# A decode step's tail: w_down's last rows laid out without zeros, the last V split elsewhere, its copy cut in three

## The chip, the cores and the metric

The kernel runs on one core of one Trainium2 chip. The core has TensorE (PE in the profile, with PEld for its weight loads), VectorE (DVE), ScalarE (ACT), GpSimd (POOL) and SyncE (SP), which here issues the transfers; 16 DMA engines move the data. The metric is the device time of one execution in microseconds (us): the median of the runs.

## The reference

One token of two batch rows (B = 2) goes through a layer norm, and then through two branches in parallel whose results are added to the input:

- attention: 32 heads of 128, each over the last W = 2048 cached positions of its own K and V. `q = xn @ wq`, `scores = q k / sqrt(128)`, softmax, `o = p @ v`, then `o @ wo` back to 512 columns.
- a gated product: `h = (xn @ w_gate) * (xn @ w_up)` with F = 1376 columns, then `h @ w_down` back to 512 columns.

```
return x + _A_ref(xn, A_k_cache, A_v_cache, A_wq, A_wo) + _B_ref(xn, B_w_gate, B_w_up, B_w_down)
```

Everything is float32. The caches and weights that are read come to 159.5 MB, each number used once or twice, so the kernel is one long stream.

## The kernel before

The host lays out all inputs as one array, `stream`, in exactly the order in which the kernel wants them (`laid_out`, line 492; `blocks`, line 41). A block is 128 partitions by so many columns, and one transfer on SyncE's queue brings one block, or one part of a block that is split. Three large buffers of 54 KB a partition (`steps`, BUFS = 3) take turns; `pump` (line 138) issues the next transfer when a buffer has been freed, and `done` (line 161) counts a buffer's fields until it is free.

Per head the work is: VectorE multiplies K by q (`products`) and sums over 128 columns (`sums`); GpSimd and ACT make the softmax weights (`maxima`, `weights`); TensorE weighs V with them (`weigh`, line 321), three heads later. `weigh` takes V in eight parts of 512 columns (2 KB a partition). Part `n` goes to batch row `n // 4` and to column group `n % 4` of the array, that is to PSUM partitions from `32 * (n % 4)`, so four parts can run side by side and two follow each other in each column group. A float32 matmul is two instructions in the profile. ACT then copies the [128, 512] result out of PSUM (`copy_out`, line 331); four matmuls with the constant `pick` gather it into a column per batch row (`transpose`, line 338; a quarter of 128 columns each, tile `tr`), ACT scales them into `oT`, and `project_o` (line 357) multiplies them by that head's rows of wo.

All results are summed in one PSUM tile, `acc`. For the last heads and the last pieces of w_down `accumulate` (line 309) splits the 512 output columns into four quarters, one for each column group: group g holds output columns 128 g to 128 g + 127 in PSUM partitions from 32 g. The lhsT has 17 columns, batch row 0 in the first and batch row 1 in the last.

`gate` (line 399), at head 3, makes h and turns it around: four rounds of one matmul into `tr` and one ACT copy into `hT`. There `hT[:, i, n]` holds h of w_down's chunk 4 n + i, a chunk being 128 rows. F = 1376 is ten chunks and 96 rows (FR = 96); `down(n)` (line 409) adds the chunks that WD lists, and line 485 adds the 96 rows. In the stream these 96 rows stand as a chunk of 128 rows of 512 columns, 32 of them zeros.

The order of the instructions on each engine is the order of the program: `InOrder` ties each to the one before it on its engine. The tail is written out by hand from line 449 on. After head 30's part: V of head 31 in two transfers, `v0` of 10 KB a partition (CL = 2560 columns, five parts) and `v1` of 6 KB; `copy_out`; `project_o(30)`; `transpose` of head 31; `down(2)`, `project_o(31)`, `down(3)`, the last 96 rows; VectorE adds x (`o_out`), and SyncE stores the result. `keep_busy(n)` (line 318) is a matmul on n columns whose result nobody reads.

Of the kernel before, what the change touches and what calls it, by code (L numbers as in the profile page):

```python
# [8 lines left out]
F32 = mybir.dt.float32  # L9
# [7 lines left out]
P = 128  # L17
B, D, H, DH, SK, F = 2, 512, 32, 128, 8192, 1376
# [3 lines left out]
FB = 4 * P  # L22
NFB = -(-F // FB)
NFC = F // P
FR = F - NFC * P
FH = [(0, 2 * FB), (2 * FB, F)]
LAG = 3
RB = 16
M = RB * (B - 1) + 1
# [3 lines left out]
CK, CQ, CO = B * J * DH, NC * GC, D  # L33
CP = CQ // NC
UNIT = CK + max(CP, CO)
STEP = 3 * UNIT
CL = CK // 2 + FB
WD = [(0, 3), (3, 5), (5, 8), (8, NFC)]


def blocks():

    def wd(n):
        return [("wd", i, D) for i in range(*WD[n])]  # L50

    def k(h):
        return [("k", h, CK)] + ([("wq", h, CP)] if h + HG < H else [])

    def v(h):
        return [("v", h, CK), ("wo", h, CO)]

    def gu(half):
        n = NC * (FH[half][1] - FH[half][0])
        return [("wg", half, n), ("wu", half, n)]  # L60

    units = []
    for h in range(LAG, H - 1):
        units += [k(h), v(h - LAG)]
    ones = [("pick", 0, 8 * B), ("rows", 0, NFB * B), ("carry", 0, M)]
    first = [("x", 0, B * NC)] + ones + [("w", 0, NC * DH)]
    loads = [[("w", 1, CQ - NC * DH)] + k(0) + k(1), gu(0) + k(2)]
    loads += [gu(1) + units[0] + units[1] + wd(0)]
    loads += [sum(units[i : i + 3], []) for i in range(2, len(units), 3)]
    loads += [k(H - 1) + v(H - 1 - LAG) + wd(1)]  # L70
    out = [(("f", 0), first)] + [(("s", i), fields) for i, fields in enumerate(loads)]
    late, last = ("s", len(loads)), ("s", len(loads) + 1)
    out += [(late, v(H - 3)), (late, v(H - 2)), (last, [("v0", H - 1, CL)])]
    out += [(last, [("v1", H - 1, CK - CL)]), (last, [("wo", H - 1, CO)] + wd(2))]
    out += [(last, wd(n)) for n in range(3, len(WD))]
    return out + [(last, [("wd", NFC, D)])]


class InOrder:
# [30 lines left out]
def kernel(  # L110
# [7 lines left out]
    pe, dve, act, sp = (InOrder(tc, e) for e in (nc.tensor, nc.vector, nc.scalar, nc.sync))  # L118
# [3 lines left out]
    const = ctx.enter_context(tc.tile_pool(name="const", bufs=1))  # L122
    steps = ctx.enter_context(tc.tile_pool(name="steps", bufs=BUFS))
    small = ctx.enter_context(tc.tile_pool(name="small", bufs=6))
# [8 lines left out]
    tiles, used, left, got = {}, {}, {}, {}  # L133
# [39 lines left out]
    rows, carry = got["rows", 0][0], got["carry", 0][0][:M]  # L173
# [12 lines left out]
    acc, acc_g = acc_t[:M, :], acc_t[:, :P]  # L186

    o_ps = [ps_c.tile([P, 4 * DH], F32, name=f"o_ps{i}") for i in range(2)]
# [15 lines left out]
    tr = ps_c.tile([P, 4 * P], F32, name="tr")  # L204
# [24 lines left out]
    n_acc = bank = 0  # L229
# [76 lines left out]
        rec_t[h] = small.tile([P, B], F32, name="rec")  # L306
        dve.reciprocal(rec_t[h], sum_t.pop(h))

    def accumulate(lhsT, rhs, last=False):
        nonlocal n_acc  # L310
        for g in range(4):
            pe.matmul(
                acc_g[32 * g : 32 * g + M, :], lhsT, rhs[:, g * P : (g + 1) * P],
                start=(n_acc == 0), stop=last,
            )
        n_acc += 1

# [13 lines left out]
    def copy_out():  # L331
        nonlocal bank
        o_sb = small.tile([P, 4 * DH], F32, name="o_sb", bufs=2)
        act.copy(o_sb, o_ps[bank])
        bank = 1 - bank
        return o_sb

    def transpose(heads, o_sb):
        d = tr[:, 8 + 4 * bank : 12 + 4 * bank]
        s0, s1 = side(heads[0]), side(heads[-1]) + 1  # L340
        dst = d.rearrange("p (s b) -> p s b", b=B)[:, s0:s1, :]
        for r in range(4):
            pe.matmul(
                dst, o_sb[:, r * DH : (r + 1) * DH], pick[:, r, s0:s1, :],
                start=(r == 0), stop=(r == 3),
            )
        for h in heads:
            rec = rec_t.pop(h)
            oT[h] = oT_ring[h % 4]
            for b in range(B):  # L350
                c = B * side(h) + b
                act.activation(
                    oT[h][:, RB * b : RB * b + 1], d[:, c : c + 1], AF.Copy,
                    scale=rec[:, b : b + 1],
                )
# [26 lines left out]
    hT = const.tile([P, 4, NFB, M], F32, name="hT")  # L382
    dve.memset(hT, 0.0)

    def project_gu(half):
        lo, hi = FH[half]
        for w, kind in enumerate(("wg", "wu")):
            t = got[kind, half][0].rearrange("p (c f) -> p c f", c=NC)
            for c in range(NC):
                for n in range(2 * half, min(2 * half + 2, NFB)):  # L390
                    f0, f1 = n * FB, min(n * FB + FB, F)
                    pe.matmul(
                        gu_ps[w][32 * n : 32 * n + B, 0 : f1 - f0],
                        xn[:, c, :], t[:, c, f0 - lo : f1 - lo],
                        start=(c == 0), stop=(c == NC - 1),
                    )
            done(kind, half)

    def gate():
        g_sb = small.tile([P, FB], F32, name="o_sb", bufs=2)  # L400
        act.copy(g_sb, gu_ps[0])
        h_sb = small.tile([P, FB], F32, name="o_sb", bufs=2)
        dve.tensor_tensor(h_sb, g_sb, gu_ps[1], op=ALU.mult)
        for i in range(4):
            t = tr[:, P + i * P // 2 : P + i * P // 2 + NFB * B]
            pe.matmul(t, h_sb[:, i * P : (i + 1) * P], rows, start=True, stop=True)
            act.copy(hT[:, i, :, ::RB], t.rearrange("p (n b) -> p n b", b=B))

    def down(n):
        for c in range(*WD[n]):  # L410
            if n < 2:
                pe.matmul(
                    acc, hT[:, c % 4, c // 4, :], got["wd", c][0],
                    start=False, stop=(c == WD[1][1] - 1),
                )
            else:
                accumulate(hT[:, c % 4, c // 4, :], got["wd", c][0])
            done("wd", c)
# [40 lines left out]
    o_sb = pv([HF])  # L459
# [16 lines left out]
    for n in range(2):  # L476
        parts = range(CL // FB) if n == 0 else range(CL // FB, CK // FB)
        weigh(H - 1, got[f"v{n}", H - 1][0], parts, True, True)
    o_sb = copy_out()
    project_o(H - 2)  # L480
    transpose([H - 1], o_sb)
    down(2)
    project_o(H - 1)
    down(3)
    accumulate(hT[:FR, NFC % 4, NFC // 4, :], got["wd", NFC][0][:FR], last=True)
    o_out = const.tile([P, P], F32, name="o_out")
    dve.tensor_tensor(o_out, acc_g, x_nat, op=ALU.add)

# [3 lines left out]
def laid_out(x):  # L492

    import numpy as np

    a = x["A_x"].reshape(B, D)
    first = {
        kind: np.zeros((P, w), a.dtype) for kind, _, w in blocks()[0][1][:4]
    }
    first["x"][:] = a.reshape(B, P, NC).transpose(1, 0, 2).reshape(P, B * NC)  # L500
    for b in range(B):
        for r in range(4):
            for s in range(2):
                first["pick"][8 * s + 4 * b + r :: 32, (2 * r + s) * B + b] = 1.0
        for n in range(NFB):
            first["rows"][32 * n + b, n * B + b] = 1.0
        first["carry"][RB * b, RB * b] = 1.0
    cache = {
        kind: x[name][:, :, SK - W :, :].reshape(B, H, P, J * DH).transpose(1, 2, 0, 3)
        for kind, name in (("k", "A_k_cache"), ("v", "A_v_cache"))  # L510
    }
    wq = x["A_wq"].reshape(P, NC, H // HG, GC).transpose(2, 0, 1, 3)
    wo = x["A_wo"].reshape(H, P, D)
    gu = {
        kind: x[name].reshape(P, NC, F)
        for kind, name in (("wg", "B_w_gate"), ("wu", "B_w_up"))
    }
    wd = np.zeros((P * (NFC + 1), D), a.dtype)
    wd[:F] = x["B_w_down"]

    def field(kind, i):
        if kind in first:
            return first[kind]
        if kind in ("k", "v"):
            return cache[kind][i].reshape(P, CK)
        if kind in ("v0", "v1"):
            v = cache["v"][i].reshape(P, CK)
            return v[:, CL:] if kind == "v1" else v[:, :CL]
        if kind == "w":
            return (wq[0][:, :, DH:] if i else wq[0][:, :, :DH]).reshape(P, -1)  # L530
        if kind == "wq":
            return wq[i // HG + 1][:, i % HG, :]
        if kind == "wo":
            return wo[i]
        if kind == "wd":
            return wd[i * P : (i + 1) * P]
        return gu[kind][:, :, FH[i][0] : FH[i][1]].reshape(P, -1)

    parts = [
        np.concatenate([field(kind, i) for kind, i, _ in fields], axis=1).ravel()  # L540
        for _, fields in blocks()
    ]
    return {
        "x_rows": a.reshape(B, D // P, P).transpose(1, 0, 2).reshape(-1, P),
        "stream": np.concatenate(parts),
    }
# [31 lines left out]
```

## Time and profile before

| | us |
|---|---|
| median of 3 runs (378.47 to 378.75) | 378.65 |
| the profiled execution | 378.59 |
| its span, from first to last instruction | 376.8 |
| VectorE busy | 293.7 (78%) |
| TensorE busy | 256.7 (68%) |
| ScalarE busy | 58.6 (16%) |
| DMA queue of the stream | 98.3% of 16 engines' span, 424 GB/s |

A row of the timeline or of a group names engine, operation, output tile, input tiles and shapes. Since the wrapper `InOrder` records all operations, nearly all rows have the same line, L94, and one goes by the tiles: `step` is a stream buffer, `o_ps` the weighed V, `o_sb` its copy, `tr` the turned columns, `oT` and `hT` the left sides of the products into `acc`. The `q<-xnb,mean_w` rows in the tail are `keep_busy`. A shape such as 128*17 128x512 means: lhsT of 128 rows and 17 columns, right side of 128 rows and 512 columns. A number in brackets is the engine's idle time before, and what ended it.

### The profile page before, as it was taken

How to read it: one execution, taken by the hardware profiler on the slowest of the kernel's cores; microseconds unless marked ns; L12 is line 12 of the kernel's file. 1: busy time of each engine (PE TensorE's matmuls, PEld its weight loads, DVE VectorE, ACT ScalarE, POOL GpSimd, SP SyncE). 2: the span in 40 equal slices, each digit the busy share in tenths (PEclk: the TensorE clock that was granted, in tenths of full speed). 3: DMA queues.
4: the chain of work that ended last, by engine and by line, in shares of the span. 5: the costliest groups of instructions: out<-in, count | busy, mean ns of one | idle time of the engine just before them, and what ended most of it. 6: DMA issues, size and time to landing. Idle time of an engine off the chain costs nothing.

```text
span 376.8 us, 2826 instructions
## 1 busy us (share of the span) xinstructions
PE 256.7 (68%) x1070; PEld 88.0 (23%) x1070; DVE 293.7 (78%) x144; ACT 58.6 (16%) x256; POOL 25.5 (7%) x78
## 2 busy tenths in 40 slices
PE   3496497987568483864848776484867638627996
PEld 3241023232122121211222221121212212012333
DVE  3299691998599499769949976994996799599940
ACT  1021001122020211202122020111202011211231
POOL 1001000000000000100000100000000000000010
PEclk9788976689686986859686786978669887666999
DMA  8999999899899998999999999999999999999995
GB/s 341 448 435 456 422 413 470 387 458 470 372 465 423 429 458 387 460 434 423 459 393 454 440 411 458 405 442 453 411 440 434 419 442 435 447 413 427 407 417 201
DMA packets 4360, 159.71 MB, mean 424 GB/s; under 512 B 492, under 2 KB 508, under 8 KB 1020
## 3 DMA queue, kind: packets, MB, share of 16 engines
q1 hardware_dynamic: 4348, 159.55, 98.3%
q8 instruction: 8, 0.13, 0.1%
q14 instruction: 4, 0.03, 0.0%
HBM read 159.54 MB, written 0.00 MB: 423 GB/s over the span
## 4 chain that ended last, share of the span: by engine, by line
DMA 63%; DVE 23%; PE 12%; ACT 1%; issue 0%; SPq 0%; DVEq 0%
DMA step<-in_stream_dram 63%; DVE step L94 12%; DVE s L94 11%; PE o_ps L94 4%; PE q L94 3%; PE acc L94 3%; PE tr L94 1%; ACT o_sb L94 1%; ACT oT L94 0%; DVE m L94 0%; SPq L94 0%; DVE o_out L94 0%; DVE rec L94 0%; ACT nm L94 0%; DVEq L94 0%
## 5 line engine op out<-in xcount | busy, mean ns | idle before, releaser
L94 DVE TENSOR_TENSOR step<-step,q 128x4096 f32<-128x4096 f32 x31 | 136.6, 4407 | 53.8 <-DMA step<-in_stream_dram 53.8
L94 PE MATMUL q<-step,xnb 128*128 128x512 f32 (+1 forms) x128 | 94.0, 885 | 74.8 <-DMA step<-in_stream_dram 74.8
L94 DVE TENSOR_REDUCE s<-step 128x32 f32<-128x4096 f32 x32 | 141.4, 4420 | 1.1
L94 PE MATMUL o_ps<-step,p 128*16 128x512 f32 x512 | 71.5, 693 | 12.0 <-DMA step<-in_stream_dram 12.0
L94 PEld LDWEIGHTS q<-step,xnb 128*128 128x128 f32 x128 | 32.8, 279 | 130.1 <-DMA step<-in_stream_dram 75.1
L94 PE MATMUL acc<-step,oT 128*17 128x512 f32 (+1 forms) x88 | 35.8, 557 | 9.3 <-ACT oT L94 8.1
L94 ACT COPY o_sb<-o_ps 128x512 f32<-128x512 f32 x24 | 14.1, 586 | 147.6 <-PE o_ps L94 147.6
L94 PE MATMUL tr<-first,o_sb 128*128 128x2 f32 (+2 forms) x192 | 26.6, 259 | 14.9 <-ACT o_sb L94 13.3
L94 PEld LDWEIGHTS tr<-first,o_sb 128*128 128x128 f32 x192 | 24.8, 198 | 36.1 <-ACT o_sb L94 32.6
L94 PEld LDWEIGHTS o_ps<-step,p 128*16 128x16 f32 x512 | 13.7, 107 | 72.9 <-issue 56.9
L287 POOL PARTITION_ALL_REDUCE mm<-m x32 | 11.4, 356 | 284.2 <-DVE rec L94 179.0
L94 ACT ACTIVATE nm<-mm 128x2 f32<-128x2 f32 x32 | 6.5, 203 | 127.7 <-POOL mm L287 127.7
L94 ACT ACTIVATE p<-s,nm 128x16 f32<-128x16 f32 x64 | 19.1, 300 | 1.0
L303 POOL PARTITION_ALL_REDUCE sum<-rs x32 | 12.8, 400 | 54.1 <-ACT p L94 54.1
L94 ACT ACTIVATE oT<-tr,rec 128x1 f32<-128x1 f32 x64 | 12.2, 260 | 27.1 <-PE tr L94 27.1
L94 PE MATMUL o_ps<-step,xn 128*2 128x512 f32 (+1 forms) x48 | 12.2, 555 | 0.0
L94 ACT ACTIVATION_READ_ACCUMULATOR p<-s,nm 128x1 f32 x64 | 11.9, 186 | 0.0
L94 DVE TENSOR_TENSOR step<-step,tr 128x4096 f32<-128x4096 f32 x1 | 4.4, 4421 | 9.2 <-DMA step<-in_stream_dram 9.2
L94 PEld LDWEIGHTS acc<-step,oT 128*17 128x17 f32 x88 | 4.9, 97 | 19.3 <-ACT oT L94 11.9
L94 PE MATMUL acc<-step,hT 128*17 128x128 f32 (+2 forms) x58 | 8.5, 368 | 0.0
L94 PE MATMUL q<-xnb,mean_w 128*128 128x512 f32 (+1 forms) x16 | 7.8, 581 | 0.0
L94 DVE TENSOR_TENSOR o_out<-acc,x_nat 128x128 f32<-128x128 f32 x1 | 0.3, 290 | 9.3 <-PE acc L94 9.3
(35 smaller groups left out, 38.5 us busy)
## 6 DMA issues: line engine op xcount, KB each, us to landing
step<-in_stream_dram SPq DMA_DIRECT2D x16, 6912.0 KB, 33.7
step<-in_stream_dram SPq DMA_DIRECT2D x2, 6400.0 KB, 32.5
step<-in_stream_dram SPq DMA_DIRECT2D x1, 6784.0 KB, 45.6
step<-in_stream_dram SPq DMA_DIRECT2D x1, 6656.0 KB, 29.2
step<-in_stream_dram SPq DMA_DIRECT2D x1, 5376.0 KB, 15.3
step<-in_stream_dram SPq DMA_DIRECT2D x1, 4864.0 KB
step<-in_stream_dram SPq DMA_DIRECT2D x2, 2304.0 KB, 17.2
step<-in_stream_dram SPq DMA_DIRECT2D x1, 1280.0 KB, 14.2
```

The lines of the kernel that those rows point to most:

```text
L94: made = call(*args, **kwargs)
L287: nc.gpsimd.partition_all_reduce(mm, m, P, bass_isa.ReduceOp.max)
L303: nc.gpsimd.partition_all_reduce(sum_t[h], rs, P, bass_isa.ReduceOp.add)
```

## The change

- The last 96 rows of w_down come as field `wr`, 128 rows of 384 columns, without zeros. Rows 0 to 95 hold their output columns 0 to 383. Rows 96 to 127 hold their output columns 384 to 511: the 96 rows are cut into three sets of 32 (FX = 32), which stand side by side.
- Line 485's four matmuls become six: for i = 0, 1, 2 one with 96 rows into column group i, and one with the 32 rows in partitions 96 to 127 into group 3.
- For these the matching parts of h are needed in partitions 96 to 127: a new tile `hX`, a memset, and three more rounds of matmul and ACT copy in `gate`.
- V of head 31 comes in parts of 12 KB and 4 KB a partition: CL = 3072 columns, six of the eight parts in `v0`.
- Head 31's `copy_out` is written out as three copies: ACT takes columns 0 to 127, VectorE 256 to 511, ACT 128 to 255, in this order in the program.
- `keep_busy(256)` stands between head 31's `transpose` and `down(2)`.

```diff
-CL = CK // 2 + FB
+CL = CK // 2 + 2 * FB
+NS = 3
+FX = FR // NS
...
-    return out + [(last, [("wd", NFC, D)])]
+    return out + [(last, [("wr", 0, NS * P)])]
...
+    hX = const.tile([P, NS, M], F32, name="hX")
+    dve.memset(hX, 0.0)
...
             pe.matmul(t, h_sb[:, i * P : (i + 1) * P], rows, start=True, stop=True)
             act.copy(hT[:, i, :, ::RB], t.rearrange("p (n b) -> p n b", b=B))
+        for i in range(NS):
+            t = tr[:, P + (2 * i + 1) * P // 4 : P + (2 * i + 1) * P // 4 + NFB * B]
+            f = (NFC % 4) * P + i * FX - FR
+            pe.matmul(t, h_sb[:, f : f + P], rows, start=True, stop=True)
+            act.copy(hX[FR:, i, ::RB], t[FR:, (NFB - 1) * B :])
...
-    o_sb = copy_out()
+    o_sb = small.tile([P, 4 * DH], F32, name="o_sb", bufs=2)
+    act.copy(o_sb[:, :DH], o_ps[bank][:, :DH])
+    dve.tensor_copy(o_sb[:, 2 * DH :], o_ps[bank][:, 2 * DH :])
+    act.copy(o_sb[:, DH : 2 * DH], o_ps[bank][:, DH : 2 * DH])
+    bank = 1 - bank
     project_o(H - 2)
     transpose([H - 1], o_sb)
+    keep_busy(256)
     down(2)
     project_o(H - 1)
     down(3)
-    accumulate(hT[:FR, NFC % 4, NFC // 4, :], got["wd", NFC][0][:FR], last=True)
+    wr = got["wr", 0][0].rearrange("p (s n) -> p s n", s=NS)
+    for i in range(NS):
+        pe.matmul(
+            acc_g[32 * i : 32 * i + M, :], hT[:FR, NFC % 4, NFC // 4, :], wr[:FR, i, :],
+            start=False, stop=True,
+        )
+        pe.matmul(
+            acc_g[32 * NS : 32 * NS + M, :], hX[FR:, i, :], wr[FR:, i, :],
+            start=False, stop=(i == NS - 1),
+        )
...
-    wd = np.zeros((P * (NFC + 1), D), a.dtype)
-    wd[:F] = x["B_w_down"]
+    wd = x["B_w_down"]
+    rest = wd[NFC * P :].reshape(FR, NS + 1, P)
...
+        if kind == "wr":
+            last = rest[:, NS, :].reshape(NS, FX, P).swapaxes(0, 1)
+            return np.concatenate([rest[:, :NS, :], last]).reshape(P, NS * P)
```

More of the change, by code (lines that the diff above doesn't have):

```diff
@@ L307, in reciprocals, with accumulate @@
         dve.reciprocal(rec_t[h], sum_t.pop(h))
-    def accumulate(lhsT, rhs, last=False):
+    def accumulate(lhsT, rhs):
         nonlocal n_acc
@@ L313, in accumulate @@
                 acc_g[32 * g : 32 * g + M, :], lhsT, rhs[:, g * P : (g + 1) * P],
-                start=(n_acc == 0), stop=last,
+                start=(n_acc == 0), stop=False,
             )
```

## The prediction

> **What bounds the kernel now.** I read the page first: how busy the DMA queue is, the chain that ended last by engine, and how long the late transfers take to land.
>
> ```profile
> span 376.8 us, 2826 instructions
> PEclk9788976689686986859686786978669887666999
> DMA  8999999899899998999999999999999999999995
> q1 hardware_dynamic: 4348, 159.55, 98.3%
> DMA 63%; DVE 23%; PE 12%; ACT 1%; issue 0%; SPq 0%; DVEq 0%
> step<-in_stream_dram SPq DMA_DIRECT2D x1, 1280.0 KB, 14.2
> step<-in_stream_dram SPq DMA_DIRECT2D x1, 768.0 KB, 15.7
> step<-in_stream_dram SPq DMA_DIRECT2D x1, 512.0 KB, 18.5
> step<-in_stream_dram SPq DMA_DIRECT2D x1, 256.0 KB, 18.6
> ```
>
> The stream fills the DMA engines for 98.3% of the span, so nothing that happens before the tail counts unless it holds back a transfer. The last slices have a full TensorE clock (9). The four one-off transfers are the last head's V in two parts and the last two pieces of w_down. In order of time they are issued at 352.89, 353.27, 354.21 and 354.69 us, so they land at about 367.1, 369.0, 372.7 and 373.3. The rest of the time is decided behind 364 us. There the chain that ended last, in order of time, has:
>
> ```profile
> 367.81 1.86 PE o_ps L94 x13
> ...
> 370.15 0.59 ACT o_sb L94
> ...
> 370.79 1.05 PE tr L94 x8
> 371.84 1.99 PE acc L94 x56
> ...
> 373.93 0.29 DVE o_out L94
> ```
>
> The chain runs over TensorE. How near the DMAs are to it is seen in the timeline of the tail, which gives start, length, engine, operation, tiles, count and the idle time before:
>
> ```profile
> 357.65 0.68 PE L94 MATMUL q<-xnb,mean_w 128*128 128x256 f32 x2
> 358.25 0.41 PE L94 MATMUL acc<-acc_sb,first 17*17 17x128 f32 x8
> 358.59 0.41 PE L94 MATMUL acc<-step,oT 128*17 128x128 f32 x8
> 358.82 1.90 PE L94 MATMUL o_ps<-step,p 128*16 128x512 f32 x16
> ...
> 371.77 0.85 PE L94 MATMUL acc<-step,hT 128*17 128x128 f32 x24
> 372.44 0.40 PE L94 MATMUL acc<-step,oT 128*17 128x128 f32 x8
> 372.78 0.35 PEld L94 LDWEIGHTS acc<-step,hT 128*17 128x17 f32 x16 [0.22 <-DMA step<-in_stream_dram]
> 373.38 0.13 PEld L94 LDWEIGHTS acc<-step,hT 96*17 96x17 f32 x8 [0.24 <-DMA step<-in_stream_dram]
> ```
>
> Both last pieces of w_down are waited for, but barely. Project_o's matmuls (four groups, two rounds of 0.11 us from 372.44) are through at 372.66, so TensorE is ahead of the DMA by only 372.78 - 372.66 = 0.12 us. A group of 128 columns takes 0.11 us per instruction in its column group, and four column groups run side by side: 24 instructions from 371.77 to 372.44 are six rounds, 0.67 / 6 = 0.11.
>
> **The change, part by part.** All times are against this profiled execution: 378.59 us, its span of 376.8 and 1.8 around it, 0.06 below the median of 378.65.
>
> *Fewer bytes.* 256 KB become 192 KB. 64 KB at the page's 424 GB/s are 0.15 us; the last landing moves from 373.34 to 373.19. That is all that the stream can give.
>
> *V in 12 and 4 KB rows.* The first part gets 256 KB more, 0.62 us, and lands at 367.74 instead of 367.1; TensorE turns to it at 367.74 before. Cost 0 to 0.05. The second part still lands at 369.0, since the sum of both is the same. Behind it stood parts 5, 6, 7, in three column groups side by side; now parts 6 and 7 in two. They take as long as three. I take 0, and the copy still starts at 370.15.
>
> *The copy in three pieces.* ACT copies take 0.17 us for 6 columns and 0.59 for 512, so 0.83 ns a column and 0.27 for 128. VectorE with an operand in PSUM takes 0.29 for 128 (o_out) and 0.69 for 512 (o_sb), so 0.42 for 256. A hand-over costs 0.05 (copy ends 370.74, transpose starts 370.79). If the pieces run side by side, the four transposes start at 370.47 and end 0.32 us earlier than now. If they take turns, the last ACT piece is there at 370.15 + 0.27 + 0.05 + 0.42 + 0.05 + 0.27 = 371.21, not 370.74. Six of eight transposes follow, the first pair being done by then: 0.25 us later than now. The nearest rows are the turns that ACT and TensorE take on one PSUM tile in the gate, although they touch different columns:
>
> ```profile
> 57.87 0.17 ACT L94 COPY hT<-tr 128x6 f32<-128x6 f32 x1 [3.02 <-PE tr L94]
> 58.09 0.39 PE L94 MATMUL tr<-first,o_sb 128*128 128x6 f32 x2 [0.25 <-ACT hT L94]
> 58.51 0.17 ACT L94 COPY hT<-tr 128x6 f32<-128x6 f32 x1 [0.48 <-PE tr L94]
> ```
>
> So I take turns: +0.25 (bounds -0.32 and +0.25). The Trainium skill, "PSUM — Partial Sum Buffer", section "PSUM bank collisions raise a hardware error", says that two engines must not touch one bank and quadrant at once, two readers included. By that rule turns are forced; no row here shows two readers.
>
> *keep_busy(256)* is new on TensorE between transposes and down(2). The row at 357.65 shows its price: from there to the next shape at 358.25 are 0.60 us, and 0.11 pass before it, the step from one transpose to the next ((1.05 - 0.25) / 7 in the row at 370.79). Now the last transpose starts at 371.59 and the first acc matmul 0.18 later. That is 0.11 + 0.60 - 0.18 = +0.54. No wait covers it: w_down's third piece has landed by 371.77. Down(2), project_o and down(3) are queued behind.
>
> Together TensorE reaches down(3) at 372.66 + 0.25 + 0.54 = 373.45 instead of waiting for 372.78. Down(3) is four rounds, 0.44, so the last product starts at 373.89, not at 373.38: **+0.51**. Its data landed at 373.19, and the 0.15 us saved is worth nothing. With the pieces side by side it starts at 372.66 - 0.32 + 0.54 + 0.44 = 373.32: -0.06.
>
> *The last product.* Before: four groups by two instructions, two rounds. Now: three times a pair with 96 rows into groups 0, 1, 2 and a pair with 32 rows, all three into group 3. Even if everything else is hidden, group 3 has six rounds instead of two: 4 x 0.11 = +0.44, the lower bound. The upper: 17-row matmuls are the only ones here that use few rows, and they are not followed at once by others. Two rounds of 17 rows take 358.59 - 358.25 = 0.34, two of 128 rows 358.82 - 358.59 = 0.23. So a change of row shape costs 0.11. The same 0.1 stands ahead of them: two instructions of 256 columns at 0.21 each leave 0.18 of the 0.60 unexplained. If the change of shape also stops other column groups, six pairs run one after another, five times 0.32 (0.34 less the 0.02 by which four groups are staggered): the last pair starts 1.6 us after the first, and the end comes +1.6. I take this, since the weights of the next shape are not loaded ahead in those rows either.
>
> Whether a change of shape stops column groups that are not concerned, these rows can't say. The Trainium skill, "TensorEngine Tiling (Array Packing)", section "Tiling Modes", says that a change of tiling mode drains the whole engine, which would be the 1.6. The Trainium skill's "TensorE: Matmul & The Clock Gate", section "Part 3: Packing small matmuls", has matmuls on different tiles start 4 ns apart, which leaves the 0.44.
>
> *The gate* gets three more rounds of two matmuls and a copy. One takes 58.73 - 58.09 = 0.64 us, up to 0.75 later, so 2.1 us on TensorE and ACT at 60 us. Behind it wait values, down(0) and with them the transfer that SyncE issues at 73.25. The DMA engines are full until 82 (share 1.14 in the window from 73 to 82), so 2.1 of some 8 us are used up: 0. VectorE's next products wait for data that land at 65.4. The memset of 51 columns lies at the start, before the first keys land: 0.
>
> **Sum:** 0.51 + 1.6 = 2.1 us on 378.59: **380.7 us** (0.55% more).
>
> **The rivals.**
> (a) Shapes stop each other, but the copies run side by side: -0.06 + 1.6, 380.1. For it: no row shows two readers taking turns.
> (b) The copies take turns, but group 3 runs beside the others: 0.51 + 0.44, 379.5. For it: column groups have queues of their own (at 369.46 a matmul of project_o runs between those of o_ps).
> (c) On the other side, not slower by what can be told: column groups don't stop each other, and the pieces run side by side, so that TensorE is back at the last landing, 373.32: -0.06 + 0.44, **379.0**. It decides if the alternating pairs cost under 0.8 us together with everything else. The gate rows speak against it.
> (d) Faster by over 0.2%: would need a stream that runs quicker as a whole; bytes give 0.15 of the 0.76 needed, and no row shows more.
> (e) Above 381.2: each change of shape waits for the results too (0.27 a matmul instead of 0.11), 0.16 x 5 = 0.8 more, 381.5.
>
> **How the numbers follow.** Forecast 0.44, (a) 0.14, (b) 0.16, (c) 0.17, (d) 0.05, (e) 0.04. Within 0.2% is about what a measurement of this kernel can tell from no change: 0.76 us, up to 379.41. Case (b) lies just over it, so I count 0.09 of it as slower and 0.07 as same. Slower 0.44 + 0.14 + 0.09 + 0.04 = 0.71; same 0.07 + 0.17 = 0.24; faster 0.05. The range must hold (b) and (c), the bounds of both unknown costs, and the forecast's own spread of 0.5: 378.9 to 381.2. The forecast's own range is 380.1 to 381.2.
>
> **What will show it.** In the tail's timeline: ACT, VectorE and ACT copies one after another from 370.15 (right) or overlapping (wrong). Down(3) with no wait for a DMA, at about 373.4. The last twelve matmuls stretched over 1.6 to 1.9 us with 96- and 32-row pairs in turn, and o_out at about 376.0 instead of 373.93. Wrong would be: 96-row pairs that start within 0.02 us of each other, or a last matmul that still waits for the stream. The DMA digits and the gate's neighbours should be as before.

## The result, and the profile after

The changed kernel takes 380.45 us (median of 6 runs, 380.27 to 381.68) against 378.63 us before (378.47 to 378.83): ratio 1.0053, 95% interval 1.004 to 1.0066. It is slower by 1.82 us, where 2.1 were forecast.

The profiled execution is the slowest of the six, 381.68 us, with a span of 379.8: its stream ran 1.2 us late already when V of head 30 landed (365.21 us, before 364.01). So stretches of the tail are compared from that landing on. From it to `o_out` are 377.00 - 365.21 = 11.79 us, before 373.93 - 364.01 = 9.92. The tail is 1.87 us longer, and that is the whole difference of the medians.

The page after, in the order of the lines shown of before:

```profile
span 379.8 us, 2854 instructions
PEclk9786988899696867868776698785969678558999
DMA  8999999999999999999999999999999999999991
q1 hardware_dynamic: 4348, 159.48, 97.5%
DMA 63%; DVE 26%; PE 8%; ACT 1%; issue 0%; SPq 0%; DVEq 0%
step<-in_stream_dram SPq DMA_DIRECT2D x1, 192.0 KB, 18.4
```

The stream still fills the DMA engines; only the last digit fell, from 5 to 1, since the end without transfers is longer. The clock is full at the end, as before. The last transfer, issued at 355.90, lands at 374.34, 9.13 us behind V of head 30; before it was 9.32. So the last data are there 0.19 us sooner, and the end is later. The chain that ended last, from V of head 30 on:

```profile
365.25 1.91 PE o_ps L97 x16
...
371.28 0.27 ACT o_sb L97
371.55 0.02 issue
371.57 0.44 DVE o_sb L97
372.01 0.02 issue
372.03 0.27 ACT o_sb L97
372.31 0.04 issue
372.35 0.83 PE tr L97 x6
373.18 0.54 PE q L97 x2
373.72 3.25 PE acc L97 x60
376.97 0.02 issue
377.00 0.29 DVE o_out L97
```

Three copies one after another (ACT, VectorE, ACT) stand where one of 0.59 stood; keep_busy (`q`) is on the chain; and the products into `acc` are one block of 3.25 us without a DMA in between. The end of that block in the timeline:

```profile
374.54 0.82 PE L97 MATMUL acc<-step,hT 128*17 128x128 f32 x18
375.29 0.11 PEld L97 LDWEIGHTS acc<-step,hX 32*17 32x17 f32 x2 [0.21 <-issue]
375.29 0.39 PE L97 MATMUL acc<-step,hX 32*17 32x128 f32 x2
375.61 0.39 PE L97 MATMUL acc<-step,hT 96*17 96x128 f32 x2
...
376.57 0.39 PE L97 MATMUL acc<-step,hX 32*17 32x128 f32 x2
```

The first row is down(3)'s 16 instructions and the first 96-row pair, which starts 4 rounds of 0.11 later, at 374.97. From there the pairs stand 0.32 us apart, up to the last at 376.57, one behind the other, though a 96-row pair and a 32-row pair write different column groups. PEld stands idle for 0.21 us ahead of the weights of each pair: they are loaded only as the pair itself starts. From 374.97 to `o_out` at 377.00 are 2.03 us; before it was 373.93 - 373.38 = 0.55.

One thing at the very end became shorter. Before, the chain had a step of VectorE's sequencer ahead of `o_out`:

```profile
373.86 0.02 DVEq L94
373.88 0.04 issue
```

In the chain after, one `issue` of 0.02 stands there. The step is absent in the traces whose tail has a VectorE copy, and there `o_out` follows the last matmul 0.07 us sooner than in a trace with one ACT copy and the same last matmul (0.305 against 0.375 us from start to start behind a 32-row matmul).

### The profile page after: what moved, and what is told of

Read it like the earlier page. It is cut to its first block, busy times and chain, and to the rows that moved or that the text cites. A ratio compares the mean times of both kernels' runs of the same rounds, so it can differ in the third digit from the quotient of the medians.

```text
span 379.8 us, 2854 instructions
## 1 busy us (share of the span) xinstructions
PE 256.9 (68%) x1082; PEld 89.1 (23%) x1082; DVE 294.1 (77%) x146; ACT 58.9 (16%) x260; POOL 25.4 (7%) x78
## 4 chain that ended last, share of the span: by engine, by line
DMA 63%; DVE 26%; PE 8%; ACT 1%; issue 0%; SPq 0%; DVEq 0%
DMA step<-in_stream_dram 63%; DVE s L97 13%; DVE step L97 13%; PE o_ps L97 3%; PE q L97 2%; PE acc L97 2%; PE tr L97 1%; ACT o_sb L97 0%; DVE m L97 0%; ACT oT L97 0%; SPq L97 0%; DVE o_sb L97 0%; DVE rec L97 0%; DVE o_out L97 0%; DVEq L97 0%
## 5 line engine op out<-in xcount | busy, mean ns | idle before, releaser
L97 PE MATMUL q<-step,xnb 128*128 128x512 f32 (+1 forms) x128 | 92.5, 873 | 77.9 <-DMA step<-in_stream_dram 77.9
L97 PE MATMUL o_ps<-step,p 128*16 128x512 f32 x512 | 70.3, 684 | 10.7 <-DMA step<-in_stream_dram 10.7
L97 PE MATMUL tr<-first,o_sb 128*128 128x2 f32 (+2 forms) x198 | 27.7, 258 | 16.0 <-ACT o_sb L97 13.2
L97 ACT COPY o_sb<-o_ps 128x512 f32<-128x512 f32 (+1 forms) x25 | 14.0, 560 | 145.6 <-PE o_ps L97 145.1
L97 PEld LDWEIGHTS tr<-first,o_sb 128*128 128x128 f32 x198 | 25.6, 197 | 37.7 <-ACT o_sb L97 32.9
L97 DVE TENSOR_REDUCE m<-s 128x2 f32<-128x32 f32 x32 | 5.9, 186 | 1.1
```

What stands on the lines that cost most here:

```text
L97: made = call(*args, **kwargs)
```

## The experiments

The theory: the slowdown is made of uncovered prices in TensorE's tail, namely five changes of row shape that stop all column groups, group 3's four extra rounds, copies that take turns, and keep_busy. The rivals are named with each run. Each is given with the kernel before run beside it (378.55 to 378.62), and medians are compared.

**The same matmuls without a change of shape.**

```diff
-            acc_g[32 * NS : 32 * NS + M, :], hX[FR:, i, :], wr[FR:, i, :],
+            acc_g[32 * NS : 32 * NS + M, :], hX[:, i, :], wr[:, i, :],
```

> The changed kernel, but the three matmuls into group 3 take all 128 rows of hX and wr; rows 0 to 95 of hX are zeros, so the sums are the same, and no matmul changes the row shape any more. My theory (a change of row shape stops all column groups, five changes): the 96-row pairs and the group 3 pairs run side by side, group 3 has six rounds of 0.11 us, the stage from the first of the last matmuls to o_out takes 0.55 + 0.44 = 1.0 us instead of 2.02, the time falls by 1.0 to 379.4. Rival (the interleaving or group 3's order itself makes the pairs wait for each other, whatever the shape): no change, 380.45.

Measured: 379.34 us, 1.11 less than the changed kernel. The tail of its timeline:

```profile
373.92 0.27 PE L97 MATMUL acc<-step,hX 128*17 128x128 f32 x1
373.93 0.36 PE L97 MATMUL acc<-step,hT 96*17 96x128 f32 x3
374.03 0.27 PE L97 MATMUL acc<-step,hX 128*17 128x128 f32 x1
374.05 0.27 PE L97 MATMUL acc<-step,hT 96*17 96x128 f32 x1
374.14 0.60 PE L97 MATMUL acc<-step,hX 128*17 128x128 f32 x4
374.78 0.29 DVE L97 TENSOR_TENSOR o_out<-acc,x_nat 128x128 f32<-128x128 f32 x1 [3.85 <-PE acc L97]
```

Same number, order and column groups, only the rows differ: now 96-row matmuls and those of group 3 start within 0.02 us of each other, and group 3 goes on by itself, 0.11 us a step. So it is not the order and not group 3's sum. A shape of 96 rows counts here as one with 128 rows, since 96*17 and 128*17 mix freely. The 32-row matmuls differ from these in place as well as in number of rows (partitions 96 to 127); the 17-row matmuls of before, in partitions 0 to 16, cost as much (0.34 us for two rounds), which speaks for the number.

**One change instead of five.** All three 96-row matmuls, then the three with 32 rows.

```diff
     for i in range(NS):
         pe.matmul(... hT[:FR, NFC % 4, NFC // 4, :], wr[:FR, i, :], ...)
+    for i in range(NS):
         pe.matmul(... hX[FR:, i, :], wr[FR:, i, :], ...)
```

> The changed kernel, but all three 96-row matmuls first and then the three 32-row matmuls: one change of row shape instead of five. My theory: 0.12 us for the 96-row pairs side by side, 0.20 for the change, then six rounds of group 3; the last matmul starts 0.9 us after the first instead of 1.72, so 0.8 us less, 379.6. Rival (each 32-row pair is slow by itself, or waits for the result of the pair before in the same group): under 0.3 us less, 380.2 or more.

Measured: 379.61 us, 0.84 less. In its timeline

```profile
374.05 0.55 PEld L97 LDWEIGHTS acc<-step,hX 32*17 32x17 f32 x6 [0.21 <-issue]
374.05 0.82 PE L97 MATMUL acc<-step,hX 32*17 32x128 f32 x6
```

the 0.21 stands once, and the six 32-row instructions take as long as 128-row ones (0.82 us for six rounds with the last one's length). Few rows are not slow; changing to them and back is.

**keep_busy away.**

```diff
     transpose([H - 1], o_sb)
-    keep_busy(256)
     down(2)
```

> The changed kernel without keep_busy(256). My theory (it stands on the path uncovered): 0.54 us less, 379.9; down(3) then starts just behind the landing of its data. Rival (it holds TensorE's clock up, and is worth its price): the granted clock falls in the last 3 us and the fifteen to thirty rounds behind it take up to twice as long, 380.5 to 382.

Measured: 379.88 us, 0.57 less. The clock does not fall without it (stretches of the tail; columns are length, each engine's busy time and instructions, granted clock, DMA share, GB/s):

```profile
372.00:374.00 2.00, 2.00 (x54) 1.38 (x46) 0.00 (x0) 0.37 (x2) 0.00 (x0) 1.00 0.14 50
374.00:375.20 1.20, 1.16 (x8) 0.33 (x6) 0.01 (x1) 0.00 (x0) 0.00 (x0) 1.00 0.00 0
```

**One copy again.**

```diff
-    act.copy(o_sb[:, :DH], o_ps[bank][:, :DH])
-    dve.tensor_copy(o_sb[:, 2 * DH :], o_ps[bank][:, 2 * DH :])
-    act.copy(o_sb[:, DH : 2 * DH], o_ps[bank][:, DH : 2 * DH])
+    act.copy(o_sb, o_ps[bank])
```

> The changed kernel with one ACT copy of 512 columns again in place of the three pieces. My theory (the pieces take turns): 0.22 to 0.25 us less, 380.2. Rival (the early start of the first transpose is worth it): no change or slower, 380.45 to 380.8.

Measured: 380.24 us, 0.21 less. In its timeline the first transpose starts 0.64 us after the copy's start, and all eight follow without a break:

```profile
370.02 0.59 ACT L97 COPY o_sb<-o_ps 128x512 f32<-128x512 f32 x1 [1.84 <-PE o_ps L97]
370.66 1.05 PE L97 MATMUL tr<-first,o_sb 128*128 128x2 f32 x8 [0.47 <-ACT o_sb L97]
```

The last transposes are what counts, and with three pieces they wait for the third. In this trace the last product starts 0.20 us sooner than in the changed kernel's (9.57 against 9.76 us behind V of head 30), and the 0.07 at `o_out` is lost again.

**The new layout alone**, on the kernel before: `blocks`, `gate`, `hX` and the six matmuls as changed; V, copy and keep_busy as before.

> The kernel before with the new layout of the last 96 rows alone (fewer bytes, the three more rounds in the gate, the six matmuls); V in 10 and 6 KB, one copy, no keep_busy. My theory: TensorE waits for the last landing, which is 0.15 us earlier, and the stage behind it is 1.47 us longer (2.02 against 0.55): 378.62 - 0.15 + 1.47 = 379.95. Rival (the gate's three rounds of 2.1 us hold back the stream): 381 or more. Rival (the shape changes only cost so much because the engine arrives late): under 379.5.

Measured: 380.02 us, 1.47 more than before. In the timeline down(3) waits for its data, as before, and the pairs alternate as in the whole change:

```profile
373.05 0.55 PEld L97 LDWEIGHTS acc<-step,hT 128*17 128x17 f32 x18 [0.27 <-DMA step<-in_stream_dram]
375.60 0.29 DVE L97 TENSOR_TENSOR o_out<-acc,x_nat 128x128 f32<-128x128 f32 x1 [10.12 <-PE acc L97]
```

The first 96-row pair starts four rounds behind 373.05, at 373.50; the stage takes 2.10 us, 1.55 more than before. The bytes give 0.14 back at the start of this stage (9.23 us behind V of head 30, before 9.37), so 1.41 at the end; the median says 0.06 more. The gate's rounds don't hold back the stream: V of head 30 lands at 364.27 here.

**All but the layout**, on the kernel before: V in 12 and 4 KB, three copies, keep_busy.

> The kernel before with everything but the new layout: V in 12 and 4 KB, the three copies, keep_busy(256); the last 96 rows as before with zeros. My theory: 0.79 us more on TensorE's path, of which the slack of 0.12 at down(3) and of 0.15 at the last piece are taken off: 0.4 to 0.5 more, 379.05. With the run before it adds up to the change's 1.82 (1.32 + 0.5). Rival (the parts interact: the whole is more than the sum of its parts): 378.7 or less.

Measured: 378.92 us, 0.37 more than before (ratio 1.0013, 1.0004 to 1.0022), just under the forecast. In its timeline no product waits for a DMA any more: 24 instructions run from 373.24 to `o_out`.

```profile
373.24 0.84 PE L94 MATMUL acc<-step,hT 128*17 128x128 f32 x24
374.14 0.29 DVE L94 TENSOR_TENSOR o_out<-acc,x_nat 128x128 f32<-128x128 f32 x1 [3.44 <-PE acc L94]
```

1.47 + 0.37 = 1.84 against 1.82 for the whole: within what these runs can tell, the two halves add up.

**V in 12 and 4 KB alone.**

```diff
-CL = CK // 2 + FB
+CL = CK // 2 + 2 * FB
```

> The kernel before with V of head 31 in parts of 12 and 4 KB alone. My theory: TensorE waits up to 0.05 us for the first part, the second lands as before and its parts run side by side; the copy starts within 0.05 us of before and the end goes by the last landing: 378.62, within 0.05. Rival (fewer parts behind the last V landing shorten the tail): 0.1 to 0.4 less.

Measured: 378.55 us, with 378.55 before beside it (ratio 1.0002, 0.9993 to 1.0011). It costs and brings nothing.

**The bytes alone**, as a transfer of 96 partitions: the last 96 rows are sent without zeros, 512 columns each, into partitions 0 to 95; the products stay as before.

```diff
-            src = stream[at : at + P * (c1 - c0)].rearrange("(p i) -> p i", p=P)
-            sp.dma_start(tiles[key][:, c0:c1], src)
+            n = rows_of(fields)
+            src = stream[at : at + n * (c1 - c0)].rearrange("(p i) -> p i", p=n)
+            sp.dma_start(tiles[key][:n, c0:c1], src)
...
```

`rows_of` gives 96 for the last field and 128 for all others.

> The kernel before with the last 96 rows as a transfer of 96 partitions by 512 columns: the same 192 KB as in the change, no zeros, no new matmul, no new round in the gate. My theory: the last landing is 0.15 us earlier and TensorE is free for it by then: 378.47. Rival (the last landing does not go by bytes, or 96 partitions are slower): 378.62 or more.

Measured: 378.75 us against 378.55 (ratio 1.0005, 0.9997 to 1.0014): not told from no change, and no gain of 0.15. The reason stands in the timeline:

```profile
373.18 0.57 PEld L98 LDWEIGHTS acc<-step,hT 128*17 128x17 f32 x24 [0.59 <-DMA step<-in_stream_dram]
```

Down(3) waits until 373.18, 9.18 us behind V of head 30, where before it started 372.78 - 364.01 = 8.77 behind. It is the transfer in front of the last that is late. The last one lands 9.45 us behind V of head 30, no sooner than the 256 KB over 128 partitions do (9.32 to 9.47 in the four traces that have them).

A 16 KB instruction load falls among the last transfers of this kernel and of the one before (the DMA queues between 369.5 and 372 us list one), and with the new layout it comes some 2 us earlier. So six idle matmuls were put into the gate, to move it in the same way.

```diff
             act.copy(hT[:, i, :, ::RB], t.rearrange("p (n b) -> p n b", b=B))
+        for _ in range(6):
+            pe.matmul(t, h_sb[:, 0:P], rows, start=True, stop=True)
```

> The kernel with the 96-partition transfer, plus six matmuls in the gate whose result is written over: they do nothing but move TensorE's instruction count, so that the 16 KB instruction load that fell at 370.3 us, among the last transfers, falls some 2 us earlier, as in the changed kernel. Theory (that load takes a DMA engine from the last pieces, and the end goes by the slowest engine): the last landing comes 0.15 to 0.3 us earlier than in the 96-partition kernel's profile, and the time is 378.35 to 378.5. Rival (96 partitions are slow by themselves, or the bytes don't count): 378.6 to 378.8 as without the shift.

> The kernel before plus the same six matmuls in the gate, bytes unchanged. Theory (the instruction load delays the last pieces): 0 to 0.15 us less than before, 378.4 to 378.55. Rival (no effect of the load's place): the time of before, within 0.05; and if the matmuls in the gate held back the stream: 379 or more.

Measured: 378.74 us with the 96 partitions, 378.52 without, against 378.57 before. The load did move in both (it lies between 367 and 369.5 us now), and neither time did. That theory falls. The transfer ahead of the last is late with the load moved too: it lands 9.01 us behind V of head 30, before 8.73. The rival's first half, that the transfer of 96 partitions goes no quicker than that of 128 with a third more bytes, fits both runs; why the transfer ahead of it lands late stays open.

**A version that might win.** If shapes cost and bytes count, the 96 rows may be sent and multiplied one place earlier, without a change of shape, so that group 3's six rounds lie in a wait. Its control has them last. In both, group 3's matmuls take 128 rows and the other three keep 96, as the timeline below shows; the expectation's "all six of 128 rows" is not what was run.

```diff
-WD = [(0, 3), (3, 5), (5, 8), (8, NFC)]
+WD = [(0, 3), (3, 5), (5, 8), (8, 9), (9, NFC)]
...
-    out += [(last, wd(n)) for n in range(3, len(WD))]
-    return out + [(last, [("wr", 0, NS * P)])]
+    return out + [(last, wd(3)), (last, [("wr", 0, NS * P)]), (last, wd(4))]
...
     for i in range(NS):
         pe.matmul(...)
+    down(4)
```

> The kernel before with the new layout of the last 96 rows, all six matmuls of 128 rows (zeros in hX, so no change of row shape), sent and multiplied one place earlier: w_down's chunk 8, the 96 rows, chunk 9. My theory (the end goes by the last landing, 64 KB sooner, and the 96 rows' six rounds of 0.11 us lie in the wait for chunk 9): 0.1 to 0.15 us less than before, 378.4 to 378.5, the first version that isn't behind the kernel before. Rival (the 0.15 us of bytes are not to be had at the end, as with 96 partitions): 378.55 to 378.75.

> The same layout and the same six matmuls of 128 rows, but last, where the change has them; V in 10 and 6 KB, one copy, no keep_busy. My theory: the last landing 0.15 us earlier, group 3's four extra rounds of 0.11 us behind it: 378.57 - 0.15 + 0.44 = 378.85; against the rows-only run (380.02) 1.1 us less, as in the whole change. Rival (the bytes give nothing): 379.0.

Measured: 378.80 us earlier (1.0007, 0.9998 to 1.0016), 378.74 last (1.0003, 0.9995 to 1.0012), 378.56 before. The control is 0.11 below its forecast, and 1.28 below the layout with changing shapes. In its trace the last product starts 0.14 sooner than before (9.23 us behind V of head 30, before 9.37): the bytes are had there, but group 3's rounds take more than that. The earlier place wins nothing, and its timeline shows why:

```profile
372.68 0.40 PE L96 MATMUL acc<-step,oT 128*17 128x128 f32 x8
372.90 0.50 PE L96 MATMUL acc<-step,hT 128*17 128x128 f32 x10
373.14 0.27 PE L96 MATMUL acc<-step,hX 128*17 128x128 f32 x1
373.14 0.37 PE L96 MATMUL acc<-step,hT 96*17 96x128 f32 x3
373.43 0.30 PE L96 MATMUL acc<-step,hT 128*17 128x128 f32 x3
373.79 0.38 PE L96 MATMUL acc<-step,hT 128*17 128x128 f32 x2
```

The wait is too short to lie in. TensorE goes from project_o (372.68) to chunk 8 (372.90) to the 96 rows (373.14) without a gap. Chunk 9 lands at 373.39, and the other groups begin their share of it at 373.43, only 0.3 us behind the start of the 96 rows. Group 3's six rounds take 0.65, until 373.79, and only then comes its share of chunk 9. Of the versions run none is faster than the kernel before by what can be told.

## Why the prediction was right, point by point

**The total.** Forecast 380.7, measured 380.45; slower by 1.82, where 2.1 were forecast. The mechanism was the one of the forecast and not that of a rival. Both terms of the sum came out 0.12 too large; neither made up for the other.

**Copies in turn: +0.25 forecast.** Shown. ACT, VectorE, ACT at 371.28, 371.57, 372.03; taking them back gives 0.21. Rival (a), pieces side by side, and half of rival (c) fall. What makes the engines take turns is a wait for the engine before:

```profile
371.57 0.42 DVE L97 COPY o_sb<-o_ps 128x256 f32<-128x256 f32 x1 [5.92 <-ACT o_sb L97]
372.03 0.27 ACT L97 COPY o_sb<-o_ps 128x128 f32<-128x128 f32 x1 [0.49 <-DVE o_sb L97]
```

That the wait is there for the PSUM tile which both read is likely, but not shown; whether the chip could stand two readers was not tried. The Trainium skill, "PSUM — Partial Sum Buffer", section "PSUM bank collisions raise a hardware error", forbids it, and the trace agrees as far as these turns go. The bound of -0.32 for copies side by side was too wide: the second quarter is ACT's second piece, there at 370.15 + 2 x 0.27 = 370.69, so six transposes could not start before 370.74, and 0.27 was the most to be had.

**keep_busy: +0.54 forecast.** Shown. Last transpose at 372.93, first product of down(2) at 373.65: 0.72 against 0.18. Without it 0.57 less, and the clock stays at 1.00. One reading behind the price of a change was wrong. I had put 0.1 of the 0.60 us from keep_busy to the 17-row matmuls down to the change of rows. Here it is 0.61 us from keep_busy (373.04) to down(2) (373.65), both with 128 rows, so no change of rows is needed for it; what both places share is lhsT's change from 128 columns to 17.

**The last product starts +0.51 later.** Mis-sized by 0.12: behind V of head 30 it starts at 374.97 - 365.21 = 9.76, before at 373.38 - 364.01 = 9.37, so +0.39. Of it, 0.07 is that the copy began sooner (6.07 behind that landing, before 6.14), where I had taken 0, and 0.04 that the turns moved the last transpose by 0.21 behind the copy's start and not by 0.25. The run with everything but the layout gives 0.37 at the end.

**The last product: +1.6, between bounds of 0.44 and 1.6.** Mechanism shown, with the distance of 0.32 us a pair as forecast. In the profile it measured 2.03 - 0.55 = +1.48, in the run with the layout alone +1.55. From the first to the last matmul's start the stage did grow by 1.58; but `o_out` follows 0.10 sooner, most of it the 0.07 of VectorE's sequencer, which is also the difference between the two runs. For the price of a change, the profile's few rows with 17-row matmuls had been enough. That it stops column groups which are not concerned was the open question, and the run without a change of shape settles it. Its stage takes 374.78 - 373.90 = 0.88 us: 1.15 of the 1.48 are the changes (1.11 by the medians), and the rest, 0.33, is group 3's four extra rounds (0.44 forecast) less the 0.10. Rival (b), at 379.5, would have been right had there been no changes: that kernel takes 379.34. The Trainium skill's rule that a change of tiling mode drains the engine ("TensorEngine Tiling (Array Packing)", section "Tiling Modes") agrees with the trace, 0.2 us from the second matmul of a pair to the next shape. The Trainium skill's rule of tiles that start 4 ns apart ("TensorE: Matmul & The Clock Gate", section "Part 3: Packing small matmuls") holds here only loosely, and only without a change of shape: 96- and 128-row matmuls on different column groups start within 0.02 us, pairs of 96 and 32 rows 0.32 us apart.

**Fewer bytes: 0.15 sooner, worth nothing.** The landing moved (9.13 against 9.32), and nobody waited for it. Right for this kernel. Where the DMA does set the end, the same bytes over 128 partitions let the last product start 0.14 sooner (the layout alone and the control), but group 3's rounds cost more than that; over 96 partitions they gave nothing.

**V in 12 and 4 KB: 0.** Shown, 378.55 against 378.55.

**The gate: 0.** Three rounds of 0.63 to 0.75 us as forecast:

```profile
61.21 0.15 ACT L97 COPY hX<-tr 32x2 f32<-32x2 f32 x1 [0.48 <-PE tr L97]
61.84 0.15 ACT L97 COPY hX<-tr 32x2 f32<-32x2 f32 x1 [0.48 <-PE tr L97]
```

TensorE turns to the next values 62.47 - 60.57 = 1.90 us behind the fourth copy into `hT`; before it was 60.00 against 60.11. That is 2.0 us more, where 2.1 were forecast. The transfer that was issued at 73.25 goes out at 73.59 and finds the engines still full (DMA share 1.08 from 73 to 82 us). In the seven other runs with these rounds V of head 30 lands at 363.92 to 364.27, before at 364.01, so the 1.2 us of the profiled execution are not the gate's.

**Cases (d) and (e).** Neither came: the stream as a whole ran no quicker, and the changes did not wait for results (0.32 a pair, not 0.48).

## What to carry to other kernels

Saving 64 KB (0.15 us of stream) is not worth six matmuls of mixed row shapes at the end: pad a stationary operand with zeros to the shape of its neighbours rather than switch, or put all matmuls of one shape together. A copy split over two engines doesn't get quicker when each piece waits for the one before, as here, where both read one PSUM tile; ask when the last piece is there, not the first. Before work is moved into a wait, look how long the engine that shall do it waits there: here it was 0.3 us, and the work took 0.65.

## What the runs showed of the hardware that was not expected

- A matmul of 96 rows mixes with 128-row ones at no cost; one of 32 rows does not, in either direction, and a pair of two float32 instructions of 128 columns then costs 0.32 us instead of 0.22. The instructions themselves are as long as with 128 rows.
- A change of lhsT from 128 columns to 17, with 128 rows on both sides, costs about as much: two instructions of 256 columns and the change take 0.61 us.
- A transfer of 192 KB over 96 partitions let its predecessor land 0.3 to 0.4 us later than the 256 KB over 128 partitions did (9.01 and 9.13 us behind V of head 30 in two traces, before 8.73); 192 KB over 128 partitions in the changed kernel landed 0.19 us sooner than the 256 KB. The cause is open.
- VectorE starts its last instruction 0.07 us sooner behind TensorE where it has made a copy 3.4 to 5.0 us before than where it has been idle for 8.6 us or more; there a step of its sequencer stands between. Why is not shown.
- A 16 KB instruction load among the last transfers can be moved by 2 us with six matmuls, and the time does not answer.
